# Zero products at the start of a Nyström attention and feed-forward kernel: narrower and 56 more, with new fetch estimates and a new written order of steps

## The chip, the cores and the metric

The kernel runs on one core of a Trainium2 chip. Five engines work side by side: TensorE (PE in the profile; its weight loads are PEld), VectorE (DVE), ScalarE (ACT), GpSimd (POOL), and SyncE (SP), which here issues nearly all DMAs. The metric is the device time of one execution in microseconds (us). A kernel's time is the median of several executions. The profile is taken from one further execution, whose span runs from its first instruction to its last.

## The reference: what is computed

Inputs are q, k and v of 8 batches, 8 heads, 576 positions and 64 numbers each, in fp32, and the weights of a feed-forward layer. The first part is attention with landmarks. The 576 positions are averaged in 32 segments, and with `sm` as a scaled softmax:

```python
A  = sm(q, k_lm)          # 576 x 32
Bm = sm(q_lm, k_lm)       # 32 x 32
C  = sm(q_lm, k)          # 32 x 576
Z  = Bm.T / (norm1(Bm) * norm_inf(Bm) + 1e-6)
for _ in range(6):
    Z = 2 * Z - Z @ Bm @ Z
x  = A @ Z @ C @ v        # then heads side by side: 8 x 576 x 512
```

The second part takes each of the 4608 rows of x, subtracts its mean, divides by its standard deviation, scales by a gain, and adds a feed-forward layer to x:

```python
out = x + relu(xn @ w_ch1) @ w_ch2     # 512 -> 2048 -> 512
```

## The kernel before, in words

Everything is one program without loops on the chip: Python writes out some 3500 products of TensorE, each with a weight load of its own, and the work of the other engines between them. A unit of attention is four heads of one batch, so a batch has two units. Batches come in sets: batch 0 alone, then (1), (2), (3, 4), (5, 6) and (7).

**The start.** SP issues the loads of q, k and v of batch 0 at once (`load`, L331, L341). While they come, `warm(11, 384)` (L1957) gives TensorE products of a tile of zeros, into a PSUM bank that nobody reads: 11 products of 128 x 128 weights and 384 columns. Then, for each of the four tiles of q and k, `turn_tile` transposes nine pieces on TensorE (pst, L326) and sums positions to landmarks by nine products with a 0/1 matrix (pm, 64 columns). Behind each tile but the last, `warm(2, 384)` (L1964) adds two more zero products. `attention0` then does batch 0: scores (psa, psc), the six iterations of Z as products of 32 x 32 blocks (st, one short group of eight an iteration, each followed by a VectorE instruction that the next group needs), the product with v (pscv), the means of the weights' rows (lesser) and the product of the result with the first weights (w,zt).

**The steps.** From there on `run()` (L1924) interleaves five streams and seven kinds of helping steps, by the written list `ORDER` (L1830). A character is a kind of step and a number behind it a count, so "2 3 43" is one step of stream 2, one of stream 3 and three of stream 4:

| sign | step |
|---|---|
| 0, 1 | attention of batches 1 to 7; sums of whole tiles on TensorE |
| 2 | first layers: a chunk of 128 hidden units (psh), a group of the weights (w,zt) |
| 3 | rows of x of batch 0 |
| 4 | second layers: products with w2 (bank<-w,hT) |
| J, M, C | transposes and sums of q and k, statistics of a row block, centred weights |
| X, W | differences of operands for the second layers of batches 4 to 7, which take seven products for eight |
| K, L | cast of a loaded tile to fp16; the next load, issued by SP |

The list has 1337 steps. What can't yet be issued is kept and issued as soon as it can be. Each engine's instructions run in the order in which they are written out, so the list sets TensorE's order, and that of SP's loads.

**The planner's clock.** While the program is written out, class `Clock` follows estimated times of all engines (`note`, L164). Steps ask it for choices: whether VectorE or ScalarE copies a result (`sooner`), whether ScalarE takes a cast from GpSimd, which of several ready pieces of attention comes next. One estimate is for TensorE's program, which comes in blocks: it takes a block to end at the 95th product (`mark`, L95) and then every 128 (`BLOCK`); the next block is taken to be asked for 16 products before the end (`LEAD`), and to be there 1200 ns and 2450 ns later, or later still when loads are queued ahead of it (L205 to L212). Attention steps with many small products look at this estimate (`calm`, L113).

Of the kernel before, what the change touches and what calls it, by code (L numbers as in the profile page):

```python
# [20 lines left out]
def kernel(  # L21
# [63 lines left out]
    class Clock:  # L85
# [78 lines left out]
        def note(self, i):  # L164
            e = str(i.engine).rsplit(".", 1)[-1]
            outs = [a.bass_ap for a in i.outs if hasattr(a, "bass_ap")]
            ins = [a.bass_ap for a in i.ins if hasattr(a, "bass_ap")]
            size = [[k for _, k in a.ap] for a in outs + ins]
            count = []
            for dims in size:  # L170
                n = 1
                for k in dims[1:]:
                    n *= k
                count.append(n)
            reads = [n for a in ins for n in keys_of(a)]
            writes = [n for a in outs for n in keys_of(a)]
            ready = 0.0
            for n in reads:
                t, who = self.wrote.get(n, (0.0, e))
                if who != e or e != "PE":  # L180
                    ready = max(ready, t + (self.WAY if who != e else 0.0))
                if n.startswith("psm"):
                    t, who = self.used.get(n, (0.0, e))
                    if who != e:
                        ready = max(ready, t + self.WAY)
            for n in writes:
                for t, who in (self.wrote.get(n, (0.0, e)), self.used.get(n, (0.0, e)),
                               (self.begun.get(n, 0.0), "")):
                    if who != e:
                        ready = max(ready, t + self.WAY)  # L190
            if type(i).__name__ == "InstDMACopy":
                start = max(self.free[e], ready)
                self.free[e] = start + (580 if e == "SP" else 100)
                half_ = size[0][0] <= 64 and any(n.startswith("stg") for n in writes)
                self.wire = (max(start + 1650, self.wire)
                             + count[0] * size[0][0] * 4 / (150.0 if half_ else 385.0))
                self.loads = self.loads[-24:] + [(start, self.wire)]
                self.issued += 1
                late_ = (1450 if self.issued <= 2 else 2030 if self.issued <= 8 else 2150 if self.issued <= 10
                         else 600 + min(2200, 0.8 * (self.wire - start - 1650)))  # L200
                done = self.wire + late_
                start = done
            elif e == "PE":
                cols = count[0]
                if self.count == self.mark - self.LEAD:  # L205
                    self.ahead = self.now()
                if self.count == self.mark:
                    self.mark += self.BLOCK
                    ready = max(ready, self.fetched)
                    asked = max(self.ahead, self.fetched - 200)  # L210
                    behind = max([w for t, w in self.loads if t <= asked] + [0.0])
                    self.fetched = max(asked + 1200, behind + 400) + 2450  # L212
                self.count += 1
                rows_, cols_ = tuple(i.tile_size)
                self.cells.append((self.now(), cols / 2.4 * rows_ * cols_ / 128 ** 2))
                if tuple(i.tile_size) == (128, 128):
                    if self.small:
                        self.free[e] = max(list(self.lanes.values()) + [self.free[e]]) + 100
                        self.small, self.lanes = False, {}
                    start = max(self.free[e], ready)  # L220
                    self.free[e] = start + max(cols / (1.2 if start < 5200 else 2.4) + 3, 56)
                    done = self.free[e] + 160
                else:
                    if not self.small:
                        self.small, self.lanes = True, {}
                        self.free[e] += 95
                    elif self.shape != (rows_, cols_):
                        self.free[e] = max(list(self.lanes.values()) + [self.free[e]]) + 85
                    self.shape = rows_, cols_
                    lane = [(a, c) for a in range(i.tile_position[0], i.tile_position[0] + rows_, 32)  # L230
                            for c in range(i.tile_position[1], i.tile_position[1] + cols_, 32)]
                    start = max([self.free[e], ready] + [self.lanes.get(x, 0.0) for x in lane])
                    self.lanes.update((x, start + max(cols / 2.4 + (19 if cols == 288 else 0), 30)) for x in lane)
                    self.free[e] = start + 4
                    done = self.lanes[lane[0]] + 160
            else:
                start = max(self.free[e], ready)
                if e == "Pool":
                    for a, z in self.locks:
                        if a <= start < z:  # L240
                            start = z
                self.ready = start
                done = start + self.took(i, e, count[0], max(count[1:] + [0]))
                self.free[e] = done - self.OVERLAP[e]
                if e == "Pool":
                    self.pool = self.pool[-8:] + [(start, done)]
                    self.free["DVE"] += sum(done - a for a, _ in self.locks[-2:] if start < a < done)
                if e == 'DVE' and count[0] == 1024 and writes[0] in parted_w1:
                    self.locks = self.locks[-4:] + [(start, done)]
            for n in reads:  # L250
                self.used[n] = max(self.used.get(n, (0.0, e)), (done, e))
                if n.startswith(("m16", "xblk")) and ":" in n:
                    name = n[:n.index(":")] + "."
                    self.begun[name] = max(done, self.begun.get(name, 0.0))
            for n in writes:
                self.wrote[n] = max(self.wrote.get(n, (0.0, e)), (done, e))
# [1563 lines left out]
    def scaled_by_pe():  # L1820
# [7 lines left out]
    begun_first = [0]  # L1828

    ORDER = (  # L1830
# [18 lines left out]
    ).split()  # L1849
    JOB, MEASURE, CENTER, MIX, MIX_W2, CAST, LOAD = range(5, 12)  # L1850

# [102 lines left out]
                break  # L1954
        assert not any(w is not None for w in waits), (order[-9:], late)

    warm(11, 384)  # L1957
    a0 = attention0()
    for w, nm in [(w, nm) for w in range(U) for nm in ("q", "k")]:
        turn_tile(w, nm)  # L1960
        if (w, nm) == (1, "q"):
            next(a0)
        if (w, nm) != (U - 1, "k"):
            warm(2, 384)  # L1964
    next(a0)
    for i in range(8):
        load_w1(i)
# [57 lines left out]
```

## Time and profile before

| what | value |
|---|---|
| time, median of 3 (lowest, highest) | 265.02 us (263.58 to 265.07) |
| the profiled execution | 264.48 us, its span 262.8 us |
| mean granted clock of TensorE | 0.987 |
| busy: PE, DVE, ACT, POOL | 253.7, 204.4, 174.0, 139.7 us |
| weight loads (PEld) | 166.5 us |
| DMA | 46.68 MB, 178 GB/s over the span |

How to read it. Busy time of an engine is the union of its instructions. Products on TensorE are pipelined and their ends are modelled, so a busy stretch can hold small gaps. The rows of digits cut the span into 40 slices of 6.57 us, each digit a share in tenths. PEclk is the share of the full clock that TensorE was granted; at 0.5 every column of a product takes twice as long. "issue" as a releaser means that an engine sat idle and no semaphore that the profile shows ended it. In a name such as `psh<-ea,m`, psh is written, ea and m are read, and a row of the timeline merges neighbours of one kind ("x8").

### The profile page before, as it was taken

What the parts mean: (1) busy time and instruction counts of PE and PEld (TensorE: products, weight loads), DVE (VectorE), ACT (ScalarE), POOL (GpSimd) and SP (SyncE); (2) the same over time, 40 slices, a digit from 0 to 9 for tenths busy, and PEclk for the clock granted to TensorE, in tenths of its full rate; (3) what the DMA queues carried; (4) which work ended last, traced back from release to release, by engine and by line L of the source; (5) the groups of instructions that cost most, each with busy time, mean ns of one, the idle gap of its engine ahead of it and who ended that gap; (6) DMA issues with size and microseconds to landing.
All of it is one profiled execution on the core that took longest, in us unless ns stands there. A gap on an engine that the chain in (4) does not pass through costs nothing.

```text
span 262.8 us, 8511 instructions
## 1 busy us (share of the span) xinstructions
PE 253.7 (97%) x3494; PEld 166.5 (63%) x3494; DVE 204.4 (78%) x466; ACT 174.0 (66%) x332; POOL 139.7 (53%) x165
## 2 busy tenths in 40 slices
PE   7879999999999999999999999999999999999994
PEld 4533665456555675455655566588888885888882
DVE  3646794899989998999987974798386889398861
ACT  2755986567866887678996769556788863786000
POOL 5197879899993499999899929600000014000000
PEclk9986999999999999999999999999999999999999
DMA  6999999998976599657971111110150006100615
GB/s 250 353 398 385 386 387 361 368 231 296 359 208 202 159 324 356 175 180 190 374 192 41 23 42 42 42 40 2 36 128 2 4 3 159 42 2 0 159 23 180
DMA packets 24174, 46.68 MB, mean 178 GB/s; under 512 B 3012, under 2 KB 3272, under 8 KB 24136
## 3 DMA queue, kind: packets, MB, share of 16 engines
q1 hardware_dynamic: 23656, 45.50, 54.2%
q10 hardware_dynamic: 480, 0.66, 0.7%
q8 instruction: 27, 0.44, 0.7%
q14 instruction: 11, 0.09, 0.1%
HBM read 36.70 MB, written 9.44 MB: 176 GB/s over the span
## 4 chain that ended last, share of the span: by engine, by line
PE 83%; ACT 5%; POOL 3%; DVE 3%; DMA 3%; issue 2%; SPq 0%; ACTq 0%; POOLq 0%; DVEq 0%
PE bank L322 53%; PE psh L322 23%; DMA stg<-in_q_dram 3%; POOL asum L316 2%; PE pscv L322 2%; ACT hT L316 1%; PE psec L322 1%; POOL ea L316 1%; PE psea L322 1%; ACT xblk L316 1%; PE psd L322 1%; ACT m L316 1%; PE psr L322 1%; ACT ea L316 1%; DVE st L316 0%
## 5 line engine op out<-in xcount | busy, mean ns | idle before, releaser
L322 PE MATMUL bank<-w,hT 128*128 128x512 f16 (+3 forms) x528 | 111.1, 334 | 0.0
L316 ACT ACTIVATE hT<-psh 128x576 f16<-128x576 f32 x126 | 79.2, 654 | 19.1 <-PE psh L322 17.8
L322 PE MATMUL psh<-ea,m 128*128 128x288 f16 x512 | 80.6, 288 | 0.7 <-DVE m L316 0.5
L322 PEld LDWEIGHTS <-hT 128*128 128x128 f16 x656 | 60.6, 98 | 28.7 <-issue 4.3
L322 PEld LDWEIGHTS <-m 128*128 128x128 f16 x512 | 49.3, 98 | 21.5 <-issue 2.1
L316 DVE SCALAR_TENSOR_TENSOR xblk<-bank,rstd,xblk 128x256 f32<-128x256 f32 (+2 forms) x77 | 38.9, 539 | 15.1 <-PE bank L322 15.0
L316 POOL TENSOR_TENSOR ea<-ea,lns 128x576 f16<-128x576 f16 x15 | 19.5, 1314 | 49.3 <-ACT lns L316 49.3
L316 POOL CAST nat<-stg 128x1152 f16<-128x1152 f32 x25 | 28.9, 1172 | 11.5 <-DVE xT L316 7.9
L316 POOL CAST natv<-stg 128x1152 f16<-128x1152 f32 (+1 forms) x17 | 19.3, 1163 | 12.5 <-DMA stg<-in_v_dram 8.7
L316 DVE BATCH_NORM_STATS2 six<-xblk 128x6 f32<-128x512 f32 x36 | 24.2, 672 | 0.1
L316 DVE STREAM_TRANSPOSE xT<-nat 128x576 uint32<-128x576 uint32 x28 | 21.2, 758 | 0.0
L316 DVE SCALAR_TENSOR_TENSOR st<-st,bank 128x128 f16<-128x128 f16 (+3 forms) x36 | 13.2, 366 | 9.3 <-PE bank L322 9.2
L322 PE MATMUL bank<-w2mix 128*128 128x256 f16 x128 | 17.4, 273 | 0.0
L322 PE MATMUL bank<-w2mix,hT 128*128 128x256 f16 x128 | 17.2, 273 | 0.0
L316 ACT ACTIVATE lns<-psd 128x576 f32<-128x576 f32 x16 | 10.3, 644 | 9.0 <-PE psd L322 8.7
L316 DVE TENSOR_REDUCE part<-xT 128x32 f16<-128x576 f16 x20 | 14.2, 741 | 0.1
L316 ACT CAST m<-bank 128x512 f16<-128x512 f32 x17 | 9.8, 591 | 6.0 <-PE bank L322 5.2
L316 ACT COPY xblk<-bank 128x512 f32<-128x512 f32 (+1 forms) x18 | 10.9, 604 | 4.3 <-PE bank L322 3.5
L316 POOL TENSOR_TENSOR asum<-asum 128x256 f32<-128x256 f32 (+1 forms) x20 | 12.8, 641 | 1.6
L322 PEld LDWEIGHTS <-st 32*32 32x32 f16 (+1 forms) x380 | 6.7, 91 | 10.9 <-DVE st L316 4.2
L322 PEld LDWEIGHTS <-w2mix 128*128 128x128 f16 x128 | 12.4, 98 | 2.0
L316 ACT ACTIVATE ec<-psec 128x256 f16<-128x256 f32 (+1 forms) x42 | 12.0, 427 | 1.5 <-PE psec L322 1.3
(133 smaller groups left out, 371.5 us busy)
## 6 DMA issues: line engine op xcount, KB each, us to landing
stg<-in_q_dram SPq DMA_DIRECT2D x16, 576.0 KB, 6.2
stg<-in_k_dram SPq DMA_DIRECT2D x15, 576.0 KB, 5.4
out_dram<-xblk SPq DMA_DIRECT2D x66, 128.0 KB, 2.5
wstg<-in_moe_w_ch_dram SPq DMA_DIRECT2D x14, 512.0 KB, 7.7
stg<-in_v_dram SPq DMA_DIRECT2D x5, 576.0 KB, 7.9
stg<-in_v_dram SPq DMA_DIRECT2D x40, 72.0 KB, 3.0
stg<-in_v_dram SPq DMA_DIRECT2D x6, 288.0 KB, 4.1
stg<-in_v_dram SPq DMA_DIRECT2D x12, 144.0 KB, 3.0
```

What stands on the lines that cost most here:

```text
L316: return lambda *args, **kw: keep(getattr(self.engine, op)(*args, **kw))
L322: keep(nc.tensor.matmul(o, l, r, start=start, stop=stop, tile_position=(rb, cb), skip_group_check=(skip or cb != 0)))
```

## The change

Three things are changed. The opening zero products become 58 of 72 columns instead of 11 of 384, and the three groups between the tiles become five of 128 columns instead of two of 384. In all there are 73 zero products instead of 17, and the later products of TensorE stand 56 places further on in its program.

In the planner, the estimate for a block asked for before 14,000 ns is 4550 ns instead of 1200, and products that share the array are taken to last 26 ns longer at 128 columns and 7 ns longer at 130.

The written order is replaced as a whole. It holds the same steps in the same numbers (830 of kind 4, 165 of 2, 117 of 0, 66 J, 36 each of M, K and L, 18 W, 11 X, 8 each of 1 and C, 6 of 3) in another sequence; only its beginning is shown.

```diff
-                    self.fetched = max(asked + 1200, behind + 400) + 2450
+                    self.fetched = max(asked + (4550 if asked < 14000 else 1200), behind + 400) + 2450
...
-                    self.lanes.update((x, start + max(cols / 2.4 + (19 if cols == 288 else 0), 30)) for x in lane)
+                    self.lanes.update((x, start + max(cols / 2.4 + (19 if cols == 288 else 26 if cols == 128 else 7 if cols == 130 else 0), 30)) for x in lane)
...
     ORDER = (
-        "2 3 4 215 3 23 M 2 J2 3 22 J3 2 1 3 2 M 22 L J 0 J 2 J 12 L 2 1 2 42 3 M 0 4 0 L 3 2 "
-        "4 2 4 2 4 0 4 03 2 4 02 M 02 4 0 4 0 4 L 0 4 K 2 42 L 43 L C 0 2 K J 2 0 42 L 4 K J "
...
+        "2 3 4 29 3 23 3 M 22 32 25 J2 23 M 22 1 J 2 J2 0 2 12 22 1 J3 L 42 0 42 0 2 4 M 4 2 "
+        "L2 0 2 4 0 L 0 2 0 3 4 M 4 04 4 0 4 0 L K 0 2 43 K 43 L 0 C 0 2 J 2 4 K 42 J2 4 K J "
...
-    warm(11, 384)
+    warm(58, 72)
     a0 = attention0()
     for w, nm in [(w, nm) for w in range(U) for nm in ("q", "k")]:
         turn_tile(w, nm)
         if (w, nm) == (1, "q"):
             next(a0)
         if (w, nm) != (U - 1, "k"):
-            warm(2, 384)
+            warm(5, 128)
```

32 rows, old and new, of the table ORDER are left out of this document.

## The prediction

> **What bounds the kernel now.** I read the page's busy line first, then its slices.
>
> ```profile
> span 262.8 us, 8511 instructions
> ...
> PE 253.7 (97%) x3494; PEld 166.5 (63%) x3494; DVE 204.4 (78%) x466; ACT 174.0 (66%) x332; POOL 139.7 (53%) x165
> ...
> PE   7879999999999999999999999999999999999994
> ...
> PEclk9986999999999999999999999999999999999999
> DMA  6999999998976599657971111110150006100615
> ...
> q8 instruction: 27, 0.44, 0.7%
> ```
>
> TensorE (PE) is busy for 97% of the span, and from the fourth slice on every digit but the last is 9. What is not 9 lies in the first three slices (20 us), and there alone the granted clock has digits below 9 (8 and 6). The profiled execution took 264.48 us: 262.8 of span and 1.7 around it. The median of the three runs, 265.02, is 0.5 above it. Next I asked who PE's products waited for; columns are total, times, longest:
>
> ```profile
> PE bank L322 <- DVE zeros L383: 1.6, 1, 1.6
> PE pscv L322 <- issue: 1.2, 1, 1.2
> PE pst L326 <- DVE nat L316: 0.8, 1, 0.8
> ```
>
> One of these waits has no releaser: 1.2 us of "issue", which no semaphore ended. The timeline of PE shows where it lies:
>
> ```profile
> 14.33 0.47 PE L322 MATMUL psc<-lm,xT 128*64 128x64 f16 x18
> ...
> 16.24 0.37 PE L322 MATMUL pscv<-natv,ect 64*64 64x130 f16 x11
> 17.82 0.48 PE L322 MATMUL pscv<-natv,ect 64*64 64x130 f16 x9 [1.22 <-issue]
> 18.23 0.29 PE L322 MATMUL bank<-st 32*32 32x64 f16 x8
> 18.46 1.03 PE L322 MATMUL bank<-w,lesser 128*128 128x512 f16 x2
> ...
> 19.59 0.61 PE L322 MATMUL bank<-w,lesser 128*128 128x512 f16 x1
> ...
> 20.94 0.63 PE L322 MATMUL bank<-w,zt 64*32 64x512 f16 x8
> 22.11 2.12 PE L322 MATMUL psh<-ea,m 128*128 128x288 f16 x8 [0.54 <-DVE m L316]
> 24.03 1.23 PE L322 MATMUL bank<-w,lesser 128*128 128x512 f16 x4
> ...
> 25.67 0.41 PE L322 MATMUL bank<-w,zt 64*32 64x512 f16 x8
> ```
>
> The same stretch in windows tells how the clock went (columns: stretch, length, busy time and instructions of PE, weight loads, DVE, ACT and POOL, granted clock, DMA share, GB/s):
>
> ```profile
> 10.76:14.17 3.41, 3.09 (x75) 1.99 (x75) 2.75 (x12) 2.88 (x6) 2.22 (x2) 1.00 0.96 309
> 14.17:17.59 3.42, 2.35 (x79) 1.40 (x80) 1.16 (x5) 2.78 (x5) 3.41 (x6) 1.00 1.06 402
> 17.59:21.00 3.41, 3.18 (x61) 1.08 (x60) 1.64 (x9) 0.00 (x0) 2.86 (x5) 0.50 1.05 387
> 21.00:24.41 3.41, 2.87 (x18) 1.21 (x18) 3.41 (x10) 2.00 (x4) 3.23 (x5) 0.50 1.06 385
> 24.41:27.83 3.42, 3.40 (x27) 1.63 (x26) 1.65 (x3) 3.26 (x6) 2.29 (x4) 1.00 1.02 383
> ```
>
> And windows of PE alone, each from the start, count its products (in brackets):
>
> ```profile
> 0.00:10.90 10.90, 8.39 (x79) 1.00 0.84 310
> 0.00:14.72 14.72, 11.88 (x170) 1.00 0.87 312
> 0.00:16.60 16.60, 13.68 (x223) 1.00 0.89 323
> 0.00:24.80 24.80, 20.12 (x295) 0.86 0.94 343
> ```
>
> The stall falls inside one row of 20 equal products (11 before it, 9 behind), exactly 223 products after the start (0.00:16.60). That is the planner's own mark for a block end: 95, then every 128. The q8 row agrees on the size: 27 packets in 0.44 MB are 16 KB each, and 6988 products and weight loads over 27 are 259 of them a packet. So I read the stall as PE's next program block arriving late. The planner takes a block to be asked for 16 products before the one ahead ends; 79 products are done at 10.90 and work goes on at 17.82, so this fetch took **6.9 us**, while loads hold the DMA engines (digit 9). The windows add the second half of the damage: in the window with the stall PE is busy for 2.35 of 3.42 us, and in the next two the clock is 0.50.
>
> **The change part by part.** *Zero products, duration.* The opening 11 of 384 columns become 58 of 72, the three groups of 2 by 384 become 5 by 128. What a narrow product costs at the early, slow clock is seen on the sums:
>
> ```profile
> 1.60 3.68 PE L322 MATMUL bank<-zeros 128*128 128x384 f16 x11 [1.60 <-DVE zeros L383]
> ...
> 6.29 0.69 PE L322 MATMUL bank<-pm,nat 128*128 128x64 f16 x9
> 6.79 0.76 PE L322 MATMUL bank<-zeros 128*128 128x384 f16 x2
> ```
>
> Nine of 64 columns from 6.29 to 6.79 are 55 ns each; scaled, 72 columns are 62 ns, and 58 of them 3.6 us against 3.68. The opening ends where it did. A group of five at 128 columns carries 640 columns instead of 768, some 0.05 us less. I count **0** for both. If narrow products took 30% longer, the 1.1 us would delay the first transposes, and the 0.8 us wait for the cast of nat (the third row of waits) takes most of it; the cost would be at most 0.3.
>
> *Zero products, count.* 58 - 11 + 3 x 3 = 56 more, so product 223 of the new program is product 167 of the old. Its fetch is asked for at new product 79: 58, nine transposes, nine sums, three zeros, which is about 7.0 us (the group at 6.79, 107 ns each at half clock). Plus 6.9 it is there at 13.9. Old product 167 runs just before 14.72, where 170 are counted: about 14.65. The margin is 0.7 us, so the **stall goes: -1.2 us**. The next block is asked for at new 207 = old 151, just before the psc group at 14.33 (152 to 169), and is there at 21.2. It is needed at new 351 = old 295, at 24.80 before and some 2.8 earlier after: 22.0. Margin 0.8; I take 0, and keep 0 to 1.0 us for a fetch that is slower here.
>
> *Half clock.* Without the stall the window 14.17:17.59 holds more work: the last nine pscv, the st products and the two lesser move into it. Its busy time rises by most of the 0.97 us in which it stood idle, to about 3.2 of 3.42, more than the 3.09 in 10.76:14.17, after which the clock stayed at 1.00. So I expect full clock. By the rows, at half and at full clock: two lesser 1.03 against 0.59, the w,zt group 0.63 against 0.41, eight psh 2.12 against 1.33, four lesser 1.23 against 1.03:
>
> ```profile
> 26.51 1.03 PE L322 MATMUL bank<-w,lesser 128*128 128x512 f16 x4
> 27.38 1.33 PE L322 MATMUL psh<-ea,m 128*128 128x288 f16 x8
> ...
> 29.70 0.59 PE L322 MATMUL bank<-w,lesser 128*128 128x512 f16 x2
> ```
>
> That is 0.44 + 0.22 + 0.79 + 0.20, and 0.22 for each of the two single lesser (19.59 and its like at 20.41): 2.1 us. Not all is on the path. DVE paces two of them:
>
> ```profile
> 18.80 0.42 DVE L316 TENSOR_TENSOR cv<-pscv,rcv 128x260 f16<-128x260 f32 x1
> ...
> 22.60 1.38 DVE L316 SCALAR_TENSOR_TENSOR m<-less,zsum,bank 128x128 f16<-128x128 f16 x4
> ```
>
> cv ends at 19.22, behind which the iteration can't move by more than 0.2 of the 0.44; the four m copies hold the psh to perhaps half of the 0.79. That leaves 1.4 to 2.1, and I take **-1.6 us**. Zero is the other end, if the clock falls all the same.
>
> [...]
>
> *What becomes of it later.* A gain at 24 us lasts if PE can go on earlier. From 24.41 on, PE waits for nothing long, and the nearest inputs behind DMA are these:
>
> ```profile
> 40.77 1.16 POOL L316 CAST natv<-stg 64x1152 f16<-64x1152 f32 x1
> ...
> 44.47 0.72 PE L322 MATMUL pscv<-natv,ecT 64*64 64x130 f16 x36
> ```
>
> natv is there at 41.93 and used at 44.47: 2.5 us of slack against a lead of 2.8. Other work fills the 0.3. Then PE is full to the end (the digits), so the lead is carried.
>
> *Fetch estimates and lane costs* (4550 for early asks; 26 and 7 ns for 128 and 130 columns) issue nothing; they only shift the planner's choices. *The written order* has the same 1337 steps, kind by kind (830 of second layers, 165 of first layers, 117 of attention, 36 loads, 36 casts), so no engine and no queue gets more work. Loads move by some ten places (the first L from place 40 to 51), with SP's issue. Their worth is unknown: a visible wait after 24.41 to be won hardly exists, so 0, between -2 (gaps under 0.15 us, which the list of waits doesn't show) and +4 (below).
>
> **Sum:** -1.2 - 1.6 = -2.8. On the profiled 264.48 that is 261.7; on the median 265.02, **262.2**, which I forecast.
>
> **The rivals.** (1) *The clock falls anyway*, since the products of the iteration are thin (st at 18.23 is 32x64): only -1.2, less up to 0.5 for the next fetch: 264. For it: busy time counts a thin product like a wide one. Against: 10.76:14.17 held the clock with 75 small products in 3.09 us. [...] (2) *The late block only moves*: if a fetch took 8 us instead of 6.9, both block ends at 14.65 and 22.0 would wait 0.4 and 0.3, and the clock may fall there: 264.5 to 265. [...] (3) *Slower: blocks end where small products run densely.* In the later attention stretches PE passes a block quickly:
>
> ```profile
> 104.10:108.70 4.60, 4.60 (x157) 1.00 0.73 225
> 151.80:155.20 3.40, 3.40 (x145) 1.00 0.35 82
> ```
>
> 128 products last 3.8 us at 104 and 3.0 at 152, and 56 products more put a block's end into each. The planner counts 3.65 us for a fetch on quiet DMA; the one above took 6.9. Where a block passes in less than its fetch takes, PE pays the difference: 0.65 us at 152 (3.65 - 3.0) and up to 3.1 at 104, where DMA is busy (6.9 - 3.8), and one fall of the clock is 2.1 more: 5.9, so 268.1. Against it: the old order met such stretches without an issue wait on PE. (4) *The order gains too*: up to 2 us, 260.3.
>
> **How the numbers follow.** The forecast's case (261.0 to 263.4) gets 0.50, (1) 0.13, (2) 0.09, (3) 0.13, (4) 0.15. One per cent, about what a measurement here tells from no change, is 262.4 and 267.7. Of the forecast's case three fifths lie below 262.4: 0.30, with (4) 0.45 faster. The rest of it, (1) and (2) make 0.42 within 1%. (3) is 0.13 slower. The range goes from 259.8, a little under (4), to 266.8, past (1) and (2); (3) stays out.
>
> **What would show it.** Right: no "issue" wait over 0.3 us on PE before 30 us; clock 1.00 from 7.35 on; the first psh some 2 us before 22.11. Rival (1): no stall, yet 0.50 between 14 and 25. (2): an issue wait at product 223 or 351. (3): issue waits at 95 + 128 k past 90 us. The forecast is wrong if the lead at 24 us is there but gone by 60, where loads at full DMA would set the pace.

## The result, and the profile after

The changed kernel took **262.78 us** (median of seven; 262.18 to 263.24) against 265.02: a ratio of 0.9924, with 0.9903 to 0.9945 as its 95% interval. That is 2.2 us, or 0.8%, less: within the 1% that the chances called "same", at its fast edge. 262.2 was forecast. The profiled execution took 262.78 us as well. Its page, with the same rows as before:

```profile
span 261.1 us, 8612 instructions
...
PE 252.0 (97%) x3550; PEld 168.4 (65%) x3550; DVE 208.3 (80%) x471; ACT 171.0 (66%) x326; POOL 140.6 (54%) x166
...
PE   7889998999999999999999999999999999999994
...
PEclk9999999999999999999999999999999999999998
DMA  7999999998956897658961101210240006100615
```

PEclk has lost its two low digits. PE has 56 instructions more and is busy for 1.7 us less. The waits of PE (total, times, longest):

```profile
PE bank L322 <- DVE zeros L382: 1.5, 1, 1.5
PE pst L326 <- DVE nat L316: 0.9, 2, 0.6
PE psh L322 <- DVE m L316: 0.9, 1, 0.9
PE bank L322 <- DVE zt L316: 0.4, 1, 0.4
PE pszc L322 <- ACT lns L316: 0.3, 1, 0.3
PE pszt L322 <- DVE st L316: 0.3, 1, 0.3
```

No row has "issue" as the releaser. Three short waits are new: bank for zt, pszc for lns, pszt for st. PE's timeline at the start, where one row of twenty pscv now runs through:

```profile
15.73 0.49 PE L322 MATMUL pscv<-natv,ect 64*64 64x130 f16 x20
16.20 0.24 PE L322 MATMUL bank<-st 32*32 32x64 f16 x8
16.37 0.60 PE L322 MATMUL bank<-w,lesser 128*128 128x512 f16 x2
...
19.43 1.68 PE L322 MATMUL psh<-ea,m 128*128 128x288 f16 x8 [0.87 <-DVE m L316]
20.95 1.03 PE L322 MATMUL bank<-w,lesser 128*128 128x512 f16 x4
```

The two lesser take 0.60 us instead of 1.03. The first eight psh start at 19.43 (22.11 before), the four lesser behind them at 20.95 (24.03 before). So 3.1 us are won by 21 us, and the span is only 1.7 shorter. The question for the runs was where the rest went.

To follow it, I laid each execution beside the profiled one of before. At each point: how much earlier (minus) or later PE had done the same amount of work, zero products left out, a product counted by its columns times its share of the array (good to about 0.1 us). The columns are times of the kernel before; the kernels are explained below.

| us | 28 | 53 | 80 | 108 | 121 | 161 | 236 |
|---|---|---|---|---|---|---|---|
| changed kernel | -3.5 | -2.6 | -2.5 | -2.0 | -1.7 | -1.7 | -1.9 |
| changed kernel, again (e12) | -3.1 | -2.3 | -2.2 | -1.7 | -1.9 | -1.8 | -1.8 |
| new program, old zeros (e10) | +0.1 | +0.5 | +1.5 | +1.8 | +1.6 | +1.7 | +1.5 |
| old program, new zeros (e9) | -3.1 | -2.6 | -2.6 | -2.5 | -2.3 | -2.0 | -2.0 |
| old program, new zeros, again (e13) | -2.9 | -2.7 | -2.7 | -2.2 | -2.3 | -2.3 | -2.3 |
| new zeros alone, planner follows (e1) | -3.1 | -2.6 | -2.6 | -2.5 | -0.9 | -0.6 | -0.3 |

Up to half a microsecond of what stands at 28 us may be chance. psa, the first product of batch 0's scores, starts at 11.55 in the profile of before, and between 10.5 and 11.3 in all others, with old and new zeros alike, as the first loads land.

### The profile page after: what moved, and what is told of

It reads as the page before. It is cut to its first block, busy times and chain, and to the rows that moved or that the text cites. A ratio compares the mean times of both kernels' runs of the same rounds, so it can differ in the third digit from the quotient of the medians.

```text
span 261.1 us, 8612 instructions
## 1 busy us (share of the span) xinstructions
PE 252.0 (97%) x3550; PEld 168.4 (65%) x3550; DVE 208.3 (80%) x471; ACT 171.0 (66%) x326; POOL 140.6 (54%) x166
## 4 chain that ended last, share of the span: by engine, by line
PE 77%; POOL 8%; DMA 6%; DVE 3%; issue 2%; ACT 2%; SPq 1%; POOLq 0%; DVEq 0%; ACTq 0%
PE bank L322 49%; PE psh L322 22%; DMA stg<-in_q_dram 5%; POOL asum L316 4%; POOL nat L316 2%; PE pscv L322 1%; DMA stg<-in_v_dram 1%; PE psd L322 1%; PE psec L322 1%; PE psea L322 1%; PE psr L322 1%; POOL ea L316 1%; ACT hT L316 1%; SPq L365 1%; SPq L331 1%
## 5 line engine op out<-in xcount | busy, mean ns | idle before, releaser
L316 ACT ACTIVATE hT<-psh 128x576 f16<-128x576 f32 x124 | 77.8, 651 | 24.8 <-PE psh L322 23.2
L316 POOL CAST nat<-stg 128x1152 f16<-128x1152 f32 x26 | 30.4, 1182 | 13.2 <-DVE xT L316 3.8
L316 ACT ACTIVATE lns<-psd 128x576 f32<-128x576 f32 x16 | 10.3, 645 | 11.7 <-PE psd L322 10.5
L316 POOL TENSOR_TENSOR asum<-asum 128x256 f32<-128x256 f32 (+1 forms) x20 | 12.2, 612 | 1.6
L316 POOL TENSOR_TENSOR asum<-nat 128x512 f32<-128x512 f16 x10 | 12.3, 1234 | 0.7
L316 ACT CAST m<-bank 128x512 f16<-128x512 f32 x16 | 9.1, 590 | 4.7 <-PE bank L322 4.6
```

The lines of the kernel that those rows point to most:

```text
L316: return lambda *args, **kw: keep(getattr(self.engine, op)(*args, **kw))
```

## The experiments

**The start alone, and the start undone.** The first kernel (e1) has the new zero products in the kernel before; the second (e3) has the old ones in the changed kernel. In both the planner sees what is issued and chooses anew.

```diff
-    warm(11, 384)
+    warm(58, 72)
...
-            warm(2, 384)
+            warm(5, 128)
```

```diff
-    warm(58, 72)
+    warm(11, 384)
...
-            warm(5, 128)
+            warm(2, 384)
```

> The kernel before with only the zero products of the change (58 of 72 columns, three groups of 5 by 128); order and estimates stay old. Theory A (the late program block and the clock behind it are the whole gain): no issue wait on PE near product 223, granted clock 1.00 from 7 to 30 us, a lead of about 3 us over the kernel before at 28 us, and 262.3 to 263.3. Theory B (the new order makes the gain): the lead at 28 us may be there, but the old order, written for a late block, loses it, and the time is above 264.3.

> The changed kernel with the old zero products (11 of 384, three groups of 2 by 384), so that the blocks end where they did; new order and new estimates stay. Theory A: the issue wait of about 1.2 us is back at product 223, the granted clock is 0.50 from about 17.6 to 24.4, and the time is 264.5 to 266. Theory B: 262.8 to 263.5, whatever the block does.

The start alone: 264.8 us, ratio 0.9985 (0.9962 to 1.0008): in the range of Theory B, though its trace has no issue wait, a clock of 1.00, and PE 3.1 us ahead at 28. The table shows the place of the loss: 1.6 us between 115 and 121. The old start under the new order: 267.41, ratio 1.0094 (1.0062 to 1.0125), above the ranges of both theories. There the stall is back, with the slow clock behind it (a row of PE's timeline; a row of windows with the columns explained in the prediction):

```profile
17.57 0.33 PE L322 MATMUL pscv<-natv,ect 64*64 64x130 f16 x9 [1.59 <-issue]
```

```profile
18.70:22.10 3.40, 2.86 (x46) 0.87 (x38) 2.63 (x11) 1.21 (x2) 2.74 (x5) 0.50 1.06 387
```

So the zero products remove the stall and the slow clock in either order. But neither kernel is the plain half of the change that its edit looks like: the planner's clock moved, and it chose other engines for some steps. The estimates alone add nothing to that: the old order with the new zeros is written out as the same program with either estimates.

**Other block positions.** Two other counts of zero products in the changed kernel: 28 more than before (e5), and 83 more (e6), of nearly the same total length.

```diff
-    warm(58, 72)
+    warm(30, 140)
```

```diff
-            warm(5, 128)
+            warm(14, 46)
```

> The changed kernel with 30 opening zero products of 140 columns instead of 58 of 72: as many columns, but block ends 28 products further on than in it (28 instead of 56 before the old place). Theory A (position against arrival): the block of product 223 is asked for at about 9.1 us, is there 6.3 to 6.9 later, and is needed at 15.2: a wait of 0.3 to 0.9 us, and 263.1 to 264.5, more if the clock falls. Rival C (the narrow products themselves, or a luckier phase of the clock's windows, made the gain): no wait, 262.8.

> The changed kernel with three groups of 14 zero products of 46 columns instead of 5 of 128: about as many columns, and block ends 27 products earlier than in it. Theory A: the block of product 223 is asked for at 7.0 us as in the changed kernel, but needed at about 12.9, before it is there (13.3 to 13.9), a wait of 0.4 to 1.0; the next is asked for at about 12.2 and needed near 18.3, a wait of 0.3 to 0.8. 264 to 265.6. Rival C (more zero products are better, or their number does not matter): no wait, 262.5 to 263.

With 28 more the wait at product 223 shrinks to 0.38 us. PE's timeline, and the window behind it, cut at the steps of its own clock:

```profile
16.03 0.33 PE L322 MATMUL pscv<-natv,ect 64*64 64x130 f16 x9 [0.38 <-issue]
```

```profile
18.86:22.27 3.41, 2.38 (x18) 1.02 (x18) 3.35 (x10) 2.03 (x4) 3.41 (x6) 1.00 1.05 387
```

The clock stays at 1.00, in this window and behind it. With 83 more nothing waits at product 223, but at product 351, a block later, there is a wait of 1.27 us, and the clock falls behind it:

```profile
18.61 0.24 PE L322 MATMUL bank<-cv,st 32*32 32x64 f16 x7 [1.27 <-issue]
```

```profile
15.36:18.77 3.41, 2.07 (x69) 0.97 (x63) 1.71 (x8) 1.02 (x2) 3.41 (x6) 1.00 1.05 394
18.77:22.18 3.41, 2.87 (x23) 1.00 (x17) 2.83 (x9) 1.70 (x3) 3.41 (x5) 0.50 1.06 388
```

So 0, 28, 56 and 83 products more give waits of 1.2 to 1.8, 0.38, none, and 1.27 a block later. That the wait is for a block can also be seen on the DMA queue of instructions, q8 (packets, MB, share). In the kernel before it moves nothing until 15.4 us and one packet from 15.4 to 16.6, where the stall begins:

```profile
q8 instruction: 1, 0.02, 5.5%
```

In the changed kernel, where product 223 stands 56 products earlier in the work, it moves nothing until 10.8 and one packet from 10.8 to 11.9:

```profile
q8 instruction: 1, 0.02, 5.4%
```

In all five kernels with such a wait (the kernel before, e3, e10, e5 and e6) the packet took about 1 us and ended 1.3 to 1.6 us before PE went on. In e6 the packet of product 223 ended at 10.92 and the product started at 12.42, about when it could; the wait of 0.4 to 1.0 us expected there did not come.

Times: 264.53, ratio 0.9981 (0.9957 to 1.0005), and 265.19, ratio 1.0003 (0.9985 to 1.0022). Rival C of both expectations, that only the narrow products or their number count, does not fit these waits. The 1.27 us is rival (2), "the late block only moves", made real by 27 products too many. Here, while the loads fill the DMA engines (a share of 1.05 and 1.06 in the three windows above), the position of a block's end is worth what such a wait costs. Both times hold more than the wait, since the planner follows. By the same comparison as in the table, PE is 1.5 us ahead at 58 and 0.4 at 80 in e5, so other choices probably cost it about a microsecond there. In e6 PE is 0.4 ahead at 28 and 1.0 behind at 80, and its executions with a mean clock of 1.00 took 264.88 and 265.54, so the clock is not most of its loss.

**A wait of another kind.** Four copies of a tile onto itself on VectorE hold up the pscv products of the changed kernel (e7); the blocks stay where they are.

```diff
-                product(range(NJ // 2, NJ))
+                product(range(NJ // 2, 6))
+                for _ in range(4):
+                    dve.tensor_copy(out=ect[0][:, 6:, :], in_=ect[0][:, 6:, :])
+                product(range(6, NJ))
```

> The changed kernel with a stall of another kind at the place of the old one: before the last 12 products of pscv of batch 0, VectorE copies a part of their input onto itself four times, one behind the other (about 1.2 us with the hand-over). No block ends there. Theory A (the clock falls because TensorE did too little in one window, whatever the reason): a wait on DVE of about 1 to 1.4 us near 15.9, and 0.50 for one or two windows of 3.4 us behind it. Rival (the fall of the clock belongs to the fetch): the wait, but 1.00 throughout.

The wait became larger than meant, 3.15 us, and the one execution took 269.91. PE's timeline, and two windows, the one ahead of the fall and the first of three at 0.50 in a row:

```profile
19.52 0.54 PE L322 MATMUL pscv<-natv,ect 64*64 64x130 f16 x12 [3.15 <-DVE ect L316]
```

```profile
14.70:18.11 3.41, 1.56 (x42) 0.75 (x41) 2.43 (x6) 2.22 (x4) 3.41 (x5) 1.00 1.06 399
18.11:21.53 3.42, 2.01 (x31) 0.79 (x31) 2.22 (x7) 0.00 (x0) 3.42 (x6) 0.50 1.05 388
```

In this one execution 0.50 followed a wait for a semaphore, as it followed the waits of 1.22 us and more for a late block, so a fetch is not needed for it. As the wait was not of the size of the others, this says nothing about how short a wait can be and still be followed by 0.50.

**The two halves without the planner's choices.** Now the zero products are exchanged while the planner still counts the others. All other instructions, and their engines, stay as they were in the old or the new program. The diff is that of e9 against the kernel before; e10 has it in the changed kernel, with the two pairs turned round.

```diff
...
+    AS_ISSUED = {(11, 384): (58, 72), (2, 384): (5, 128)}
     def warm(n, cols):
         idle = banks.take([P, 512])
+        n_, cols_ = AS_ISSUED.get((n, cols), (n, cols))
+        for _ in range(n_):
+            i = nc.tensor.matmul(idle[:, 0:cols_], zeros[:, 0:P], zeros[:, 0:cols_], start=True,
+                                 stop=True, tile_position=(0, 0), skip_group_check=False)
+            tc.keep_in_program_order(i)
         for _ in range(n):
-            MM(idle[:, 0:cols], zeros[:, 0:P], zeros[:, 0:cols])
+            ap = [SimpleNamespace(bass_ap=x) for x in (idle[:, 0:cols], zeros[:, 0:P], zeros[:, 0:cols])]
+            clock.note(SimpleNamespace(engine=i.ins.engine, outs=ap[:1], ins=ap[1:], tile_size=(128, 128)))
```

> The program of the kernel before, instruction by instruction on every engine, with only the zero products of the change in place of its own; the planner is not told of them, so that it chooses as it did. It differs from the run with the start alone in one thing: the cast of q's third tile of batches 5 and 6 stays on ScalarE, where that run has it on GpSimd. Theory D (that run lost 1.6 us of its lead between 115 and 121 us since the cast of 1.2 us made GpSimd, which is on the chain there, later): the lead is still 2 us or more at 121, and the time is 262.4 to 263.4. Rival E (GpSimd's chain there lasts as long as it lasts, and an order written for a later start has nothing to fill with): the lead falls to about 0.9 at 121 as in that run, and the time is 264.3 to 265.

> The program of the changed kernel, instruction by instruction, with only the old zero products (11 of 384, three groups of 2 by 384); the planner is not told of them. The late block and the half clock come back, so that nothing is left of the lead at 28 us. Theory F (the new order as such is as good as the old): the lead stays near 0 to the end, 264.8 to 265.6. Rival G (the new order as such loses the 1.7 us that the changed kernel loses of its lead after 28 us, whenever it starts): 266.3 to 267.

The old program with the new zeros: 263.4 us, ratio 0.9948 (0.9922 to 0.9974). It is below e1, which differs from it by the engine of one cast (and the place of one VectorE instruction near 154 us); the intervals overlap a little, but that of the repeat (e13, below) does not overlap e1's. The old zeros in the new program: 266.19, ratio 1.0057 (1.0031 to 1.0084), between the two ranges and nearer to Rival G. Its stall is that of the kernel before, and half a microsecond longer (PE's timeline):

```profile
17.84 0.33 PE L323 MATMUL pscv<-natv,ect 64*64 64x130 f16 x9 [1.76 <-issue]
```

But the table shows more: level with the old order at 28 us, it falls 1.5 us behind by 80. (e3, where the planner chose anew, loses as much there, and by the same comparison another 1.7 us between 149 and 161.) **With the old zeros the new order is slower by itself**, and in the stretch where the changed kernel loses its lead. Two of the waits there are the ones that the list of the changed kernel had new (PE's waits in e10, then the place in the changed kernel's timeline):

```profile
PE bank L323 <- DVE st L317: 0.8, 3, 0.4
...
PE bank L323 <- DVE zt L317: 0.4, 1, 0.4
PE pszt L323 <- DVE st L317: 0.3, 1, 0.3
```

```profile
44.27 0.22 PE L322 MATMUL bank<-st 32*32 32x32 f16 x8
44.82 0.24 PE L322 MATMUL pszt<-st,cv 32*32 32x32 f16 x16 [0.34 <-DVE st L316]
44.89 0.22 PE L322 MATMUL pszc<-cv,st 32*32 32x64 f16 x8
45.51 0.39 PE L322 MATMUL bank<-w,zt 64*32 64x512 f16 x1 [0.41 <-DVE zt L316]
```

This is the end of an iteration of Z, a chain of short products and VectorE instructions. The old order puts two pairs of bank<-w,hT, 0.60 us each, between its links; the new one puts none. PE's timeline in e9, which has the old order:

```profile
44.50 0.22 PE L323 MATMUL bank<-st 32*32 32x32 f16 x8
44.66 0.60 PE L323 MATMUL bank<-w,hT 128*128 128x512 f16 x2
45.19 0.24 PE L323 MATMUL pszt<-st,cv 32*32 32x32 f16 x16
45.26 0.21 PE L323 MATMUL pszc<-cv,st 32*32 32x64 f16 x8
45.40 0.60 PE L323 MATMUL bank<-w,hT 128*128 128x512 f16 x2
45.93 0.39 PE L323 MATMUL bank<-w,zt 64*32 64x512 f16 x1
```

Between 44 and 50 us PE loses 0.7 us against the kernel before in the changed kernel, e12 and e10, and 0.2 or less in e9 and e13; the 0.34 and 0.41 us account for that. The rest, up to 80 us, I didn't take apart.

**Why the new zeros gained nothing in e1.** The choice by which e1 differs from e9 is where a tile of q of batches 5 and 6 is cast: ScalarE in e9, GpSimd in e1. GpSimd's timeline in e9 and in e1, from these casts to the products with lns (reciprocals of the softmax sums, made by ScalarE, by which GpSimd multiplies ea):

```profile
103.11 2.23 POOL L317 CAST nat<-stg 128x1152 f16<-128x1152 f32 x2
...
112.30 2.53 POOL L317 TENSOR_TENSOR ea<-ea,lns 128x576 f16<-128x576 f16 x2
```

```profile
103.25 3.33 POOL L316 CAST nat<-stg 128x1152 f16<-128x1152 f32 x3
...
113.68 2.53 POOL L316 TENSOR_TENSOR ea<-ea,lns 128x576 f16<-128x576 f16 x2
```

And ScalarE's third lns<-psd behind them, which started at 115.92 in the kernel before (waiting for PE there). First e9, then e1, then the changed kernel:

```profile
113.62 0.65 ACT L317 ACTIVATE lns<-psd 128x576 f32<-128x576 f32 x1 [0.43 <-POOL ea L317]
```

```profile
115.00 0.65 ACT L316 ACTIVATE lns<-psd 128x576 f32<-128x576 f32 x1 [1.84 <-POOL ea L316]
```

```profile
114.34 0.65 ACT L316 ACTIVATE lns<-psd 128x576 f32<-128x576 f32 x1 [0.83 <-POOL ea L316]
```

With PE two to three microseconds ahead, GpSimd's sums, casts and products are what comes last here, even in e9 by 0.43 us. One more cast on GpSimd (1.1 us) makes the lns 1.4 us later, and PE then waits 0.6 and 1.0 us for lns (the waits of PE in e1):

```profile
PE pszc L322 <- ACT lns L316: 1.0, 1, 1.0
...
PE pszt L322 <- ACT lns L316: 0.6, 1, 0.6
```

The changed kernel casts three there on GpSimd too. So I moved that one cast to ScalarE in the changed kernel (e11), and let the planner go on counting it on GpSimd:

```diff
...
-            if by_act:
+            if (self.bs, nm, w) == ((5, 6), "q", 2):
+                tc.keep_in_program_order(nc.scalar.copy(t[:], stg[:]))
+                clock.note(InstTensorCopy(engine="Pool", outs=[SimpleNamespace(bass_ap=t[:])],
+                                          ins=[SimpleNamespace(bass_ap=stg[:])]))
+            elif by_act:
                 scalar.copy(t[:], stg[:])
```

> The changed kernel with one instruction moved: the cast of q's third tile of batches 5 and 6 on ScalarE instead of GpSimd, all else as it was. Theory D: the changed kernel's wait on ScalarE's lns at 116 us (0.3) goes, its lead does not fall between 115 and 121 us, and the time is 262.2 to 262.6. Rival E: no difference, or ScalarE's copies come later by as much, 262.8 to 263.6.

Both expectations missed: 263.98, ratio 0.9967 (0.9942 to 0.9993), no better and probably worse than the changed kernel. ScalarE's timeline, and GpSimd's:

```profile
106.01 1.15 ACT L1114 CAST nat<-stg 128x1152 f16<-128x1152 f32 x1
```

```profile
107.31 1.16 POOL L321 TENSOR_TENSOR asum<-nat 128x512 f32<-128x512 f16 x1 [3.29 <-ACT nat L1114]
...
114.21 2.53 POOL L321 TENSOR_TENSOR ea<-ea,lns 128x576 f16<-128x576 f16 x2
```

ScalarE came to the cast at 106.01 only, and GpSimd, which sums that tile next, stood still for 3.29 us. Its products with lns began at 114.21 instead of 113.02. In e9 ScalarE did the same cast at 103.31. So the engine is not the point: GpSimd's chain must not be held up, by a cast of its own or by another engine's late one.

**The changed kernel and the old program with new zeros, side by side.** Both once more on one chip: the first is e12, the second, e9 again and unchanged, is e13.

> The changed kernel once more, beside the next run on the same chip. As before: a ratio of about 0.992 to the kernel before, 262.6 to 263.2.

> The program of the kernel before with the new zero products alone once more, on the same chip as the changed kernel. Theory H (the new order adds nothing to the new zeros; its 1.6 us of loss after 28 us, seen with the old zeros, stands against 0.4 us that it gains before, and the old program loses 1.1 there): both within 0.4 us of each other, as their profiled spans (261.1 and 260.8) say. Rival I (the new order is needed and adds about 0.6 us, as the ratios 0.9924 and 0.9948 of two different jobs say): this one is slower by 0.5 to 1.0 us.

262.78, ratio 0.9933 (0.9901 to 0.9965), and 262.72, ratio 0.9917 (0.9889 to 0.9945): the same, within what this can tell. With the choices of engines held, the parts of the change are then:

| ratio to the kernel before | old zeros | new zeros |
|---|---|---|
| old order, old estimates | 1 | 0.9948, 0.9917 |
| new order, new estimates | 1.0057 | 0.9924, 0.9933 |

New zeros in the new program are worth 1.2 to 1.3%, or 3.3 to 3.5 us; in the old program 0.5 to 0.8%, or 1.4 to 2.2 us. The new order and estimates cost 0.6% with the old zeros, and nothing measurable with the new ones. No kernel here beats both by a measurable amount.

## Why the prediction was right or wrong

**The late block: right.** "The stall goes" (-1.2): no issue wait is left, and the waits with 0, 28, 56 and 83 products more go with the packets of q8. In the changed kernel the packet ends at 11.80; 1.3 to 1.6 us behind it is 13.1 to 13.4, and product 223 starts at 14.07. That leaves 0.7 to 1.0 us, where 0.7 was claimed. The fetch was no fixed 6.9 us, though: from product 79 (207 in e6) to the end of the wait it took 6.6 to 7.5 us where PE waited, and by the same working about 6.0 to 6.3 in the changed kernel. The planner's 95 and 128 fit the waits at products 223 and 351. That a block is asked for 16 products before the end of the one ahead, and the 3.65 us with which rival (3) reckons, are the planner's numbers too, and no run tests them. "The next block: 0" was right as well: its packet ends at 18.38 and product 351 starts at 21.60, so the margin was 1.6 to 1.9 us and not 0.8. With 27 products more it waits for 1.27 us.

**The zero products' duration at 0: right.** The 58 take 3.66 us against 3.68 for the 11, and a group of five 0.44 at full clock against 0.49:

```profile
1.47 3.66 PE L322 MATMUL bank<-zeros 128*128 128x72 f16 x58 [1.47 <-DVE zeros L382]
```

**The half clock at -1.6: it goes, and by about that much.** The windows of the changed kernel, two cut as those of before and one as the steps of its own clock lie:

```profile
14.17:17.59 3.42, 3.31 (x113) 1.62 (x107) 2.00 (x9) 2.45 (x4) 3.42 (x6) 1.00 1.06 397
17.59:21.00 3.41, 2.54 (x42) 1.10 (x32) 3.26 (x11) 1.83 (x3) 3.27 (x5) 1.00 1.04 387
...
17.23:20.64 3.41, 2.52 (x40) 0.94 (x40) 3.08 (x11) 1.47 (x3) 3.33 (x4) 1.00 1.05 392
```

The first has 3.31 us of work (3.2 forecast). But the clock's own steps lie elsewhere in each execution (here at 17.23 and 20.64, in the kernel before at 17.59 and 21.00), and the window behind, which the forecast didn't look at, has only 2.52. It is nearer to the 2.35 of the kernel before, so the comparison of 3.2 with 3.09 left out the window with the least work in it. That it matters where the steps happen to lie is an estimate of mine, from 2.52 and 2.35, that no run tests. (In the page of before, the low clock digit 6 stands in the fourth slice, not in the first three; the windows have it right.) What 0.50 costs is seen on the lesser of the kernel before: one more in a row took 0.42 us at 0.50 (1.03 for two at 18.46, 0.61 for one at 19.59) and 0.22 at 1.00 (1.03 for four at 26.51, 0.59 for two at 29.70). The sum for the start was -2.8; the table has -2.9 to -3.5 at 28 us, up to 0.5 of it perhaps from the first loads. The cleanest pair is e10 and e12, one program with either zeros: +0.1 and -3.1, a difference of 3.2, of which e10's wait is 1.76; 1.4 are left for the clock. The times of the kernel before say nearly the same. Of the 70 executions that were timed beside the experiments, 4 kept a mean clock of 0.999 to 1.000 and took 263.1 to 263.9 us, and the 41 with 0.984 to 0.987 took 264.4 to 265.6, by the medians of a chip 1.6 to 1.7 us more. Only their times and clocks are on record, so whether the block also came earlier in the four stays open. Rival (1) is out: 1.00 stands in all three windows. Cut at each clock's own steps, some 3.4 us apart, the clock fell behind windows in which PE was busy for 2.35 us (the kernel before), 2.07 (e6), 1.77 (e3), 1.59 (e10) and 1.56 (e7), and held behind 2.52 (here), 2.38 (e5, e9) and 2.36 (e13). Falls and holds lie too close together for a limit to be read from this.

**"So the lead is carried": wrong for the old program.** Of 2.9 to 3.1 us at 28, 2.0 to 2.3 reach the end in e9 and e13, and 0.3 in e1. The step looked at inputs behind DMA and at PE's fullness. It did not ask which engine would come last once PE was early. In e1 that is GpSimd between 97 and 118 us, and 1.6 us go there. In e9 and e13 only 0.3 to 0.4 us go between 80 and 121; 0.2 to 0.5 are gone by 53 already, and e9 loses 0.3 behind 121, for causes that no run took apart. What the step feared first, loads, did take the slack: natv is ready at 41.61 now and used at 41.56 by the modelled start, where 2.5 us lay between before. It cost nothing that the waits show.

```profile
40.45 1.16 POOL L316 CAST natv<-stg 64x1152 f16<-64x1152 f32 x1
```

```profile
41.56 0.78 PE L322 MATMUL pscv<-natv,ecT 64*64 64x130 f16 x36
```

**The written order, estimates and lane costs at 0: wrong as a term, by +1.5 us** (e10), inside the -2 to +4 that was kept. That they issue nothing was right, and that waits of PE after 24.41 hardly exist to be won was too. What was not weighed is that the order can make new ones, as at 44.8 us. The changed kernel's loss of 0.9 to 1.0 us between 28 and 80 goes with this term; it is there without any lead (e10). **The sum:** -2.8 forecast; by the medians -2.2 measured, by the ratio -2.0. Taken in the new program it is -3.3 to -3.5 for the zeros, where -2.8 was forecast, and +1.5 for the order, where 0 was: a term too small by 0.5 to 0.7 and a missing loss that outweighs it. The two errors have opposite signs, so that the total came within 0.6 us is in part luck. Rival (3), blocks that end in dense stretches, didn't happen: no issue wait past 90 us. Rival (4), the order gains too, fell with e10, and with the new zeros e12 and e13 show no gain.

What stays open: why the new order costs 1.5 us with the old zeros and nothing measurable with the new ones. In the table the lead under the new order is 3.2 us at 28 (e12 against e10) and 3.3 at the end, so none is lost at GpSimd's chain, where the old program loses 0.3 to 0.4; what in the order makes that so, no run isolates. Nor is it settled which of the planner's estimates turns which choice in e1, e3 and e5.

## What to carry to other kernels

A wait on TensorE that no semaphore ends, at a fixed count of products, can be moved by the mere number of products ahead of it (here 1.22 us at product 223 was gone with 56 more); look at the next block end too, since the same shift moves it (with 83 more nothing waited at 223, and 1.27 us at 351). Before a head start is counted to the end, ask at each join which other engine will come last once TensorE is early, and whether its slack is as large as the lead. Where a planner chooses engines while the program is written, an edit at the start is never that edit alone: hold the choices fixed to measure it.

## What the runs showed of the hardware that was not expected

In the profiled executions a late program block cost twice or not, by size: a wait of 0.38 us (e5) left the clock at 1.00, and waits of 1.22 to 1.76 were followed by two windows, 6.8 us, at 0.50. Behind the 3.15 us for VectorE (e7) there were three. The packet of a late block took about 1 us, and PE went on 1.3 to 1.6 us behind its end, so of the 6.6 to 7.5 us, counted from where the planner takes it to be asked for, 4.2 to 4.9 had passed before the packet began. And the landing of the first loads moves the start of psa by 1.0 us between executions (10.53 in e9, 11.55 in the kernel before; the cast that waits for the third load starts at 7.64 and 8.66); of the 0.6 between e9 and e13 (11.15), 0.2 is left at 28 us. A lead read from two single profiles at the start is no surer than that.
